# First gate weights loaded as words into the room of later tiles, and an opening written as one fixed list

## The chip, the cores and the metric

One NeuronCore of a Trainium2 chip runs the whole kernel. The metric is the device time of one launch in microseconds (us), taken as the median of several executions. Engines are named as in the profile: PE does the matmuls and the transposes through the identity, DVE the elementwise work on vectors, ACT the activations and copies, POOL little but the issue of loads, and SP issues most transfers.

## The reference

The three weight matrices are 64-bit floats, all other inputs 32-bit floats. There are 8 batches, 8 heads, 576 tokens and a head size of 64. Each head's keys and values are first condensed into 32 memory slots by a softmax over the tokens; the queries then attend to the 32 slots; the 4608 x 512 result goes through a gated feed-forward layer of width 1536.

```python
a = softmax(phi, axis=tokens)                     # (b, h, s, 32)
k_m = einsum('bhsm,bhsd->bhmd', a, k)             # 32 slots a head
v_m = einsum('bhsm,bhsd->bhmd', a, v)
attn = softmax(q @ k_m.T / 8) @ v_m               # (b, h, s, 64)
x = attn as (4608, 512)
out = (sigmoid(x @ w_gate) * (x @ w_val)) @ w_out # 512 -> 1536 -> 512
```

## The kernel before

**Weights.** The weights lie in memory as 64-bit words, two 32-bit integers each. The kernel turns them into 32-bit floats on the chip. `magnitude` lets ACT take the absolute value of the upper halves (L185), and `to_f32` then runs four DVE operations (L194 to L201): a clamp, a shift and mask, and two that put sign, exponent and low bits together. The 1536 columns are cut into twelve tiles f of 128. For each f there are three conversions of 128x512 numbers: (f, 0) and (f, 1) are the halves of the joint w_gate and w_val tile `wg[:, f]`, (f, 2) is the w_out tile, which is also split into `wo_hi` and `wo_lo` (L218 and L125). The words go through four rotating buffers named `words`. `CONVERT` says at which step each conversion is due; `load_jobs` issues the next load as soon as a buffer is free, by SP's queue in the opening and by POOL's later.

**Attention of one batch b.** `a_max` and `a_exp` make the softmax numerators of phi in place. `memory(b)` turns them by PE (nine transposes, copied by ACT into a tile named `e` and into `tails`), multiplies them with the keys and values `kvm` and `kvt` into one PSUM bank (80 small matmuls), scales by the reciprocal sums and turns the result into `kT` and `vT`. `scores` multiplies queries and `kT` for a cut c of the tokens (256 or 320), and DVE turns the result (L350). `s_max`, `s_exp` and `normalize` are the softmax on blocks of 32, `turned` turns it back (L396, L399), and `turn_hi` and `turn_lo` split it into `at_hi` and `at_lo`, each rounded so that three products hi-hi, hi-lo and lo-hi make up a full one.

**Feed-forward.** `make_u(b, fs)` multiplies `vT` with one or two tiles of `wg`, so that values and gate weights are joined, and splits the product into `u_hi` and `u_lo`. `gate_half(b, f, c)` then does twelve matmuls of `u` with `at` (gate and value, two halves, three products), ACT's sigmoid, DVE's product (L491), and its split into `g_hi` and `g_lo`. `out_half(b, f, c)` multiplies these with w_out into up to four accumulators `acc`, three half steps behind (LAG = 3). For batches 0 to 3 the tiles are done four at a time: steps 0 to 3 are batch 0 with tiles 0 to 3, steps 4 to 7 batch 1, steps 8 to 11 batch 2, steps 12 to 15 batch 3; then come batches 0 to 3 with tiles 4 to 7, then 8 to 11. After each four, sums go to memory as `part`. Batches 4 to 7 run through all twelve tiles at once.

**Order.** Matmuls keep their order in the program (`in_turn`), and so do table-bound activations (`curve`) and the transfers of each queue (`move`). A `step` or `piece` is put behind all that stands in the list so far, on PE, DVE, ACT and POOL. In the opening (L627 to L678) whole functions are listed, with `warm(n)` between them: n matmuls of the identity into a bank nobody reads. From step 0 on the loop at L755 works through the steps, and generators from `sides` run the attention of the next batch beside them. The opening ends with the second half of step 0; batch 1's attention lies beside steps 0 to 3, batch 2's beside steps 4 to 7, batch 3's beside steps 8 to 11. PSUM has eight banks: four `pu_t` in rotation, four `acc`, of which three join the rotation while the opening runs (`spread`).

Of the kernel before, what the change touches and what calls it, by code (L numbers as in the profile page):

```python
# [52 lines left out]
def attn_moe_kernel(
# [133 lines left out]
    def to_f32(f, k):  # L187


        if (f, k) not in sized:  # L190
# [10 lines left out]
        last_conv[0] = nc.vector.scalar_tensor_tensor(  # L201
            bits, low, 29, bits, op0=ALU.logical_shift_right, op1=ALU.bitwise_or
        )
# [7 lines left out]
        load_jobs(queue="batch" if spread else "stream")  # L211
        return dst

    def convert(f, k):
        dst = to_f32(f, k)
        if k == 2:
            hi, lo = wo_of(f)
            nc.scalar.copy(hi, dst)  # L218
# [49 lines left out]
    def memory(b):  # L268


        ph, z = loaded.pop((b, "phi")), loaded.pop((b, "z"))
        pf = ph.rearrange("p g s -> p (g s)")
        am = att([P, 2 * S], "e")[:, : NG * SF * P]
        am = am.rearrange("p (g c x) -> p g c x", g=NG, c=SF)
        for g in range(NG):
            pt = bank().rearrange("p (c x) -> p c x", c=SF)
            for c in range(SF):
                o = (g * (SF + 1) + c) * P
                transpose(pt[:, c, :], pf[:, o : o + P], ident)
            nc.scalar.copy(am[:, g], pt)  # L280
            yield
        pt = bank()
        transpose(pt[:, :P], pf[:, SF * P : (SF + 1) * P], ident)
        for g in range(NG):
            gs = slice(g * TAIL, (g + 1) * TAIL)
            nc.scalar.copy(tails[gs, g, :], pt[gs, :P])
        yield
        rz = att([P, NG], "rz")
# [1 line left out]
        nc.vector.reciprocal(rz, z)  # L290
        km, kt = loaded.pop((b, "kv"))
        kvp = bank().rearrange("p (g w d) -> p g w d", g=4, w=2)
        for g in range(NG):
# [20 lines left out]
        kvT = bank().rearrange("p (w g x) -> p w g x", w=2, g=NG)
        for g in range(NG):
            for w in range(2):
                transpose(kvT[:, w, g, :], kb[:, g, w].rearrange("p j d -> p (j d)"), ident)
        kvTs[b] = [keep.tile([P, NG, P], F32, name=f"{w}T", bufs=5 if w == "v" else 1) for w in "kv"]
        for w in range(2):
            nc.scalar.copy(kvTs[b][w], kvT[:, w])  # L320
# [107 lines left out]
    def make_u(b, fs):  # L428

# [7 lines left out]
        hi, lo = u_tiles()  # L437
        for r in range(2):
            nc.scalar.copy(hi[:, r, :nf], pb[r])  # L439
# [25 lines left out]
    def gate_half(b, f, c):  # L465
        hi, lo = U[b, f]
# [24 lines left out]
        last_prod[0] = nc.vector.tensor_tensor(prod[:, :n], ps[1][:, :n], sg[:, :n], op=ALU.mult)  # L491
# [354 lines left out]
```

## Time and profile before

| | |
|---|---|
| Time, median of three | 788.45 us (785.35 to 788.77) |
| Profiled execution, its own time | 786.25 us |
| Span of the profiled execution | 784.5 us |
| PE busy | 745.7 us (95%) |
| DVE busy | 436.6 us (56%) |
| ACT busy | 336.2 us (43%) |
| First gate matmul on PE | 30.64 us after the span's start |
| Begin of step 8 (batch 2) on PE | 121.95 us |

A group row gives source line, engine, operation, output and inputs with shapes, the count, the busy time and mean of one in ns, and the idle time of the engine ahead of it with what ended it. A timeline row gives start, duration, engine, line, operation and tiles, and in brackets the idle time ahead. A stage row gives, for a stretch of the span, its length, each engine's busy time and count, PE's granted clock, the share of the DMA engines and the rate in GB/s.

### The profile page before, as it was taken

The page shows a single profiled execution, that of the slowest core. Times are in us where ns is not written, and L with a number is a line of the kernel's source. Part 1 is how long each engine was busy: PE and PEld are TensorE (multiplying, and loading weights), DVE is VectorE, ACT ScalarE, POOL GpSimd, SP SyncE. Part 2 cuts the span into 40 slices and gives each one's busy share as a digit, 9 for nine tenths or more (in the row PEclk, how much of TensorE's full clock was granted, in tenths as well). Part 3 has the DMA queues.
Part 4 walks back from the last instruction along what each step waited for, and adds up shares of the span by engine and source line. Part 5 has one row for each costly group of instructions (what it writes and reads, how often), then busy time and mean ns, then how long its engine had stood idle before and what let it go on. Part 6 is the DMA issues. An engine that isn't in the chain of part 4 may idle for free.

```text
span 784.5 us, 13851 instructions
## 1 busy us (share of the span) xinstructions
PE 745.7 (95%) x5658; PEld 613.1 (78%) x5658; DVE 436.6 (56%) x840; ACT 336.2 (43%) x789; POOL 15.8 (2%) x34
## 2 busy tenths in 40 slices
PE   6866999989999999999999999999999999999997
PEld 4645777768888888887788878878888888888886
DVE  2889566977577775445554654365234553343432
ACT  3446455545544434332533443346333443333422
POOL 0001000001000000000000000000000000000000
PEclk8998899999999999999999999999999999999999
DMA  9683545664845654333253133002000100010002
GB/s 344 239 307 123 199 178 203 222 224 155 283 171 195 192 204 164 112 108 114 68 199 145 58 104 122 1 28 86 3 1 2 54 14 1 1 55 1 1 1 67
DMA packets 31231, 93.17 MB, mean 119 GB/s; under 512 B 3520, under 2 KB 4544, under 8 KB 29120
## 3 DMA queue, kind: packets, MB, share of 16 engines
q1 hardware_dynamic: 22528, 69.22, 24.4%
q0 software_dynamic: 4032, 14.68, 5.6%
q10 hardware_dynamic: 4608, 8.39, 3.6%
q8 instruction: 44, 0.72, 0.4%
q14 instruction: 19, 0.16, 0.1%
HBM read 69.73 MB, written 22.54 MB: 118 GB/s over the span
## 4 chain that ended last, share of the span: by engine, by line
PE 77%; DVE 9%; ACT 6%; DMA 4%; issue 2%; SPq 0%; ACTq 0%; DVEq 0%; POOLq 0%
PE pu_t L135 47%; PE acc L135 30%; DMA words<-in_wgv_dram 2%; ACT L110 2%; ACT ph L110 1%; DVE u_lo L125 1%; DVE q L396 1%; DVE e L375 1%; DVE sg L491 1%; DVE e L360 1%; ACT sg L110 1%; DVE at_lo L125 1%; DMA part<-row 1%; DMA out_dram<-row 1%; ACT e L110 1%
## 5 line engine op out<-in xcount | busy, mean ns | idle before, releaser
L135 PE MATMUL pu_t<-at_hi,u_hi 128*128 128x256 f32 (+1 forms) x760 | 229.1, 301 | 7.2 <-ACT u_hi L439 3.9
L135 PE MATMUL pu_t<-at_hi,u_lo 128*128 128x256 f32 (+1 forms) x760 | 225.0, 296 | 3.2 <-DVE u_lo L125 3.2
L135 PE MATMUL pu_t<-at_lo,u_hi 128*128 128x256 f32 (+1 forms) x760 | 225.2, 296 | 1.6 <-DVE at_lo L125 1.6
L491 DVE TENSOR_TENSOR sg<-pu_t,sg 128x256 f32<-128x256 f32 (+1 forms) x190 | 86.7, 456 | 202.8 <-ACT sg L110 129.6
L110 ACT ACTIVATE sg<-pu_t 128x256 f32<-128x256 f32 (+1 forms) x190 | 78.2, 412 | 224.3 <-PE pu_t L135 209.1
L135 PEld LDWEIGHTS pu_t<-at_hi,u_hi 128*128 128x128 f32 x760 | 144.2, 190 | 19.7 <-ACT u_hi L439 4.8
L135 PE MATMUL acc<-wo_hi,g_hi 128*128 128x512 f32 x384 | 157.1, 409 | 0.2 <-DVE row L517 0.2
L135 PE MATMUL acc<-wo_hi,g_lo 128*128 128x512 f32 x384 | 151.2, 394 | 0.0
L135 PE MATMUL acc<-wo_lo,g_hi 128*128 128x512 f32 x384 | 151.2, 394 | 0.0
L135 PEld LDWEIGHTS pu_t<-at_lo,u_hi 128*128 128x128 f32 x760 | 144.4, 190 | 8.3 <-DVE at_lo L125 1.8
L135 PEld LDWEIGHTS pu_t<-at_hi,u_lo 128*128 128x128 f32 x760 | 144.2, 190 | 4.1 <-DVE u_lo L125 4.1
L492 ACT CAST g_hi<-sg 128x256 fp32r<-128x256 f32 x192 | 78.0, 406 | 126.3 <-DVE sg L491 120.3
L125 DVE TENSOR_TENSOR g_lo<-sg,g_hi 128x256 fp32r<-128x256 f32 x192 | 80.9, 422 | 58.8 <-ACT g_hi L492 58.8
L135 PEld LDWEIGHTS acc<-wo_hi,g_hi 128*128 128x128 f32 x384 | 72.5, 189 | 49.5 <-issue 39.4
L135 PEld LDWEIGHTS acc<-wo_hi,g_lo 128*128 128x128 f32 x384 | 72.4, 189 | 17.2
L135 PEld LDWEIGHTS acc<-wo_lo,g_hi 128*128 128x128 f32 x384 | 72.5, 189 | 8.6
L125 DVE TENSOR_TENSOR u_lo<-pu_t,u_hi 128x512 fp32r<-128x512 f32 (+1 forms) x100 | 63.3, 663 | 3.6 <-ACT u_hi L439 2.3
L135 PE MATMUL pu_t<-wg,vT 64*32 64x512 f32 (+1 forms) x800 | 59.2, 596 | 5.8 <-DVE wg L201 5.2
L439 ACT CAST u_hi<-pu_t 128x512 fp32r<-128x512 f32 (+1 forms) x100 | 51.8, 570 | 2.6 <-PE acc L135 1.0
L517 DVE TENSOR_TENSOR row<-acc,row 128x512 f32<-128x512 f32 x32 | 21.9, 686 | 6.7 <-DMA row<-part 5.6
L110 ACT ACT_TABLE_LOAD x18 | 23.1, 1283 | 1.7 <-PEq L836 0.7
L135 PEld LDWEIGHTS pu_t<-wg,vT 64*32 64x32 f32 x800 | 10.3, 105 | 17.1 <-DVE wg L201 7.0
(93 smaller groups left out, 579.8 us busy)
## 6 DMA issues: line engine op xcount, KB each, us to landing
kvm<-in_kvm_dram SPq DMA_DIRECT2D x16, 1024.0 KB, 7.5
q<-in_qT_dram SPq DMA_DIRECT2D x16, 512.0 KB, 5.4
part<-row SPq DMA_DIRECT2D x32, 256.0 KB, 2.3
row<-part ACTq DMA_DIRECT2D x32, 256.0 KB, 2.8
out_dram<-row SPq DMA_DIRECT2D x32, 256.0 KB, 2.0
words<-in_wgv_dram POOLq DMA_DIRECT2D x12, 512.0 KB, 5.3
words<-in_wo_dram POOLq DMA_DIRECT2D x10, 512.0 KB, 5.2
ph<-in_phiT_dram SPq DMA_DIRECT2D x8, 576.0 KB, 4.0
```

Of the source, the lines that this page charges most:

```text
L110: last_act[0] = nc.scalar.activation(*args, **kw)
L125: return nc.vector.tensor_tensor(lo, x, hi.bitcast(F32), op=ALU.subtract)
L135: last_pe[0] = do(*args, **kw)
L360: nc.vector.tensor_tensor(e, e, mx.unsqueeze(3).broadcast_to([P, 2, w, M]), op=ALU.subtract)
L375: nc.vector.tensor_tensor(e, e, zs.unsqueeze(3).broadcast_to([P, 2, w, M]), op=ALU.mult)
L396: nc.vector.transpose(t.rearrange("p r n -> p (r n)"), loaded[b, "e"])
L439: nc.scalar.copy(hi[:, r, :nf], pb[r])
L491: last_prod[0] = nc.vector.tensor_tensor(prod[:, :n], ps[1][:, :n], sg[:, :n], op=ALU.mult)
L492: nc.scalar.copy(ghi, prod[:, : 2 * P])
L517: nc.vector.tensor_tensor(st, o, st, op=ALU.add)
```

## The change

Three things change.

First, the words of the w_gate tiles 0 to 3 no longer go through the `words` buffers. `load_gate(f)` loads all 1024 KB of a tile at once into `wg[:, 4 + 2f : 6 + 2f]`, the room of two later tiles, which is empty then. `gate_size` (ACT) and `gate_bits` (DVE) convert from there, tile 0 in two halves, tiles 1 to 3 in one go of 1024 columns. The w_out tiles 0 to 3 keep the four buffers.

Second, functions are split by engine (`scores` into `scores_of` on PE and `scores_turn` on DVE, `gate_half` into five, `make_u` into three, `memory` into its parts, and so on), and one text, `OPENING`, lists all operations of the steps 0 to 7, with the attention of batches 0 to 2, the first maximum of batch 3, the loads and the warm-ups. The loop begins at step 8. For batches 1 and 2 the phi numerators and the scaled keys get tiles of their own (`rooms`, three buffers of `left`) in place of `e`. U is made for two tiles at a time from the start.

Third, the conversions of tiles 4 to 6 are due at steps 11 to 15, up to two a step; before they were due at steps 7 to 15, one a step. From step 16 on nothing is moved.

```diff
+FIRST = 4
 CONVERT = {
-    -1: [(0, 0), (0, 1), (1, 0), (1, 1)], 0: [(0, 2), (2, 0), (2, 1)],
-    1: [(1, 2), (3, 0), (3, 1)], 2: [(2, 2)], 3: [(3, 2)], 7: [(4, 0)], 8: [(4, 1)], 9: [(4, 2)],
-    10: [(5, 0)], 11: [(5, 1)], 12: [(5, 2)], 13: [(6, 0)], 14: [(6, 1)], 15: [(6, 2)],
+    11: [(4, 0)], 12: [(4, 1), (4, 2)], 13: [(5, 0), (5, 1)], 14: [(5, 2), (6, 0)], 15: [(6, 1), (6, 2)],
...
+FIRST_U = [(0, [0, 1]), (0, [2, 3]), (1, [0, 1]), (1, [2, 3]), (2, [0, 1])]
+OPENING = """
+out 0; phi 0; gate 0; gate 3; gate 2; kvm 0 0; kvt 0; gate 1; kvm 0 1; ws 0; wb 0; amax 0; wh 0; wl 0;
+sz 0 0; sz 0 1; bt 0 0; aexp 0; bt 0 1; sz 3; W 42; T 0 0; T 0 2; T 0 1; Z 0; A 0 2; bt 3; phi 1;
+A 0 1; q 0 0; sz 2; q 0 1; A 0 0; W 23; K 0 0; bt 2; sz 1; bt 1; W 28; K 0 1; B 0; kvt 1; kvm 1 0;
+kvm 1 1; amax 1; W 5; t 0; V 0 0; V 0 1; W 2; S 0 0; aexp 1; U 0 0; tr 0 0; mx 0 0; S 0 1; uh 0 0;
+T 1 1; T 1 0; Z 1; A 1 1; T 1 2; ul 0 0; phi 2; A 1 0; q 1 0; A 1 2; out 3; ex 0 0; tr 0 1; q 1 1; W 7;
+K 1 0; out 2; nm 0 0; kvm 2 0; mx 0 1; W 8; K 1 1; B 1; kvm 2 1; tn 0 0; kvt 2; amax 2; ex 0 1; W 5;
+t 1; hi 0 0; V 1 0; nm 0 1; aexp 2; W 6; S 1 0; V 1 1; W 5; T 2 2; lo 0 0; T 2 1; A 2 2; S 1 1; tn 0 1;
+A 2 1; G 0 0 0; Z 2; hi 0 1; tr 1 0; lo 0 1; T 2 0; tr 1 1; U 0 2; sg 0 0 0; mx 1; A 2 0; G 0 0 1;
+uh 0 2; sg 0 0 1; G 0 1 0; gm 0 0 1; gm 0 0 0; ul 0 2; K 2 0; ex 1; G 0 1 1; gh 0 0 0; nm 1; K 2 1;
+sg 0 1 0; gh 0 0 1; G 0 2 0; B 2; kvt 3; out 1; gm 0 1 0; gl 0 0 0; gh 0 1 0; U 1 0; gl 0 0 1;
+sg 0 1 1; gl 0 1 0; sg 0 2 0; gm 0 1 1; G 0 2 1; uh 1 0; gm 0 2 0; tn 1; gh 0 1 1; t 2; sg 0 2 1;
+ul 1 0; G 0 3 0; hi 1; gm 0 2 1; V 2 0; O 0 0 0; lo 1; ws 1; V 2 1; G 0 3 1; gl 0 1 1; q 2 1; gh 0 2 0;
+wb 1; phi 3; sg 0 3 0; kvm 3 0; q 2 0; O 0 0 1; gl 0 2 0; wh 1; gm 0 3 0; G 1 0 0; sg 0 3 1; wl 1;
...
+"""
...
+    def early_words(f):
+
+        return wg[:, FIRST + 2 * f : FIRST + 2 * f + 2].rearrange("p f k n -> p (f k n)").bitcast(I32)
+
+    def load_gate(f):
+        move(early_words(f), wgv[f].rearrange("p k n -> p (k n)").bitcast(I32))
+
+    def gate_cut(f, k):
+
+        cut = slice(0, 1024) if k is None else slice(k * 512, k * 512 + 512)
+        words = early_words(f).rearrange("p (n t) -> p n t", t=2)
+        return wg[:, f].rearrange("p k n -> p (k n)")[:, cut], words[:, cut]
+
+    def gate_size(f, k=None):
+        dst, words = gate_cut(f, k)
+        nc.scalar.activation(dst, words[:, :, 1].bitcast(F32), AF.Abs)
+
+    def gate_bits(f, k=None):
+        last_conv[0] = bits_of(*gate_cut(f, k))
...
+    rooms.update(dict.fromkeys((1, 2), [mb.tile([P, TURN, P], F32, name="left", bufs=6) for _ in range(NG + 1)]))
+    halves = [mb.tile([P, 1024], F32, name=f"u_{w}", bufs=2) for w in ("hi", "lo")]
     warm(24)
-    step(a_max, 0)
-    step(a_exp, 0)
-    step(convert, 0, 0)
-    piece(m0, 3)
-    warm(8)
...
+    for word in OPENING.replace("\n", ";").split(";"):
+        if not word.split():
+            continue
+        name, *args = word.split()
+        if name == "O":
+            spread.clear()
+        ACTIONS[name](*map(int, args)) if name == "W" else step(ACTIONS[name], *map(int, args))
...
     sides = {
-        0: ([3, 3, 3, 2, 2, 1], m1, load(load_phi, 2), score(1, 2, load(load_kv, 2)), attend(1)),
-        begin[1, 0]: ([3, 3, 2, 2, 2, 1], remember(2, True), score(2, 3), attend(2)),
         begin[2, 0]: ([3, 3, 2, 2, 2, 1], remember(3, True), score(3), attend(3)),
...
+    pend = [(1, f, c, False, f == 3) for f in (2, 3) for c in range(2)][-LAG:]
     for i, (b, f, at_start, at_end) in enumerate(steps):
+        if i < DONE:
+            continue
```

In the list, `sz` and `bt` are the two parts of a w_gate conversion, `ws`, `wb`, `wh` and `wl` those of a w_out tile; `amax`, `aexp`, `T`, `A`, `Z`, `K`, `B`, `t` and `V` belong to the memory slots; `S`, `tr`, `mx`, `ex`, `nm`, `tn`, `hi` and `lo` to the attention; `U`, `uh` and `ul` to U; `G`, `sg`, `gm`, `gh` and `gl` to a gate half; `O` is an output half, `E` its copy from PSUM, `W n` are n warm-up matmuls, and `out`, `phi`, `gate`, `kvm`, `kvt`, `q` and `more` are loads. The numbers are batch, tile and cut. The part left out goes on in the same way to the last product of step 7, with w_out 2 and 3, batch 2's scores and softmax, and at its end the loads of batch 3's queries and keys.

More of the change, by code (lines that the diff above doesn't have):

```diff
@@ L210, in to_f32 @@
             pools["conv"] = ctx.enter_context(tc.tile_pool(name="conv1", bufs=1))
-        load_jobs(queue="batch" if spread else "stream")
+        load_jobs()
         return dst
@@ L266, in a_exp @@
         loaded[b, "z"] = z
[L268 to L288, printed above, removed]
-        nc.vector.tensor_scalar_add(z, z, EPS)
[L290 to L293, printed above, removed]
+    rooms = {}
@@ new lines, in phi_turn, with phi_copy @@
+    def phi_turn(b, g):
+        pf = loaded[b, "phi"].rearrange("p g s -> p (g s)")
+        pt = loaded[b, "pt", g] = bank()
+        for c in range(SF) if g < NG else range(1):
+            o = (g * (SF + 1) + c) * P if g < NG else SF * P
+            transpose(pt[:, c * P : (c + 1) * P], pf[:, o : o + P], ident)
+    def phi_copy(b, g):
+        pt = loaded.pop((b, "pt", g))
+        if g == NG:
+            for g in range(NG):
+                gs = slice(g * TAIL, (g + 1) * TAIL)
+                nc.scalar.copy(tails[gs, g, :], pt[gs, :P])
+            return
+        if (b, "am") not in loaded:
+            am = rooms.get(b)
+            if am is None:
+                am = att([P, 2 * S], "e")[:, : NG * SF * P].rearrange("p (g c x) -> p g c x", g=NG, c=SF)
+                am = [am[:, i] for i in range(NG)]
+            loaded[b, "am"] = am
+        nc.scalar.copy(loaded[b, "am"][g], pt.rearrange("p (c x) -> p c x", c=SF))
@@ L294, in memory, with phi_sum, keys @@
+    def phi_sum(b):
+        z = loaded.pop((b, "z"))
+        loaded[b, "rz"] = att([P, NG], "rz")
+        nc.vector.tensor_scalar_add(z, z, EPS)
+        nc.vector.reciprocal(loaded[b, "rz"], z)
+    def keys(b, gs=range(NG)):
+        am, kt = loaded[b, "am"], loaded[b, "kvt"]
+        if gs[0] == 0:
+            loaded[b, "kvp"] = bank().rearrange("p (g w d) -> p g w d", g=4, w=2)
+        kvp = loaded[b, "kvp"]
+        for g in gs:
+            km = loaded.pop((b, "kvm", g))
             for c in range(SF + 1):
@@ L312, in memory, with keys_turn, keys_keep @@
             )
-        yield
[L314 to L320, printed above, removed]
+        loaded[b, "kb"] = kb
+    def keys_turn(b):
+        kb = loaded.pop((b, "kb"))
+        kvT = loaded[b, "kvT"] = bank().rearrange("p (w g x) -> p w g x", w=2, g=NG)
+        for w in range(2):
+            for g in range(NG):
+                transpose(kvT[:, w, g, :], kb[:, g, w].rearrange("p j d -> p (j d)"), ident)
+    def keys_keep(b, ws=range(2)):
+        kvT = loaded[b, "kvT"]
+        if ws[0] == 0:
+            kvTs[b] = [keep.tile([P, NG, P], F32, name=f"{w}T", bufs=5 if w == "v" else 1) for w in "kv"]
+        for w in ws:
+            nc.scalar.copy(kvTs[b][w], kvT[:, w])
+    def memory(b):
+        for g in range(NG):
+            phi_turn(b, g)
+            phi_copy(b, g)
+            yield
+        phi_turn(b, NG)
+        phi_copy(b, NG)
+        yield
+        phi_sum(b)
+        keys(b)
+        yield
+        keys_copy(b)
+        yield
+        keys_turn(b)
+        keys_keep(b)
         yield
@@ L402, in turn_hi @@
     def turn_hi(b, c, t):
-        if not c:
+        if b not in at:
             new_at(b)
@@ L428, in make_u, with u_banks @@
     def make_u(b, fs):
+        u_banks(b, fs)
+        u_hi(b, fs)
+        u_lo(b, fs)
+    def u_banks(b, fs):
         nf = len(fs)
@@ L501, in out_half, with out_of @@
     def out_half(b, f, c, at_start, at_end):
+        out_of(b, f, c, at_start, at_end)
+        if at_end:
+            out_end(b, f, c)
+        if (b, f + 1) in ends and c:
+            for t in range(2):
+                rows[b, t] = row_of(b, t)
+    def out_of(b, f, c, at_start, at_end):
         hi, lo = G.pop((b, f, c))
```

248 lines of the change are left out of this document (144 added, 104 removed).

## The prediction, written before the result was known

> **What bounds the kernel now.** I read the page's slices first, then a table of busy time by stage.
>
> ```profile
> span 784.5 us, 13851 instructions
> ...
> PE   6866999989999999999999999999999999999997
> ...
> DVE  2889566977577775445554654365234553343432
> ```
>
> PE is full from the fifth slice on, but for one slice and the last, so only the front can give much; there DVE is the fuller engine.
>
> ```profile
> core 0: us, PE busy (x) PEld busy (x) DVE busy (x) ACT busy (x) POOL busy (x), PEclk, DMA share, GB/s
> 0.00:20.80 20.80, 13.25 (x161) 9.85 (x169) 4.17 (x9) 7.21 (x16) 0.70 (x6) 0.84 0.93 344
> 20.80:30.60 9.80, 6.17 (x77) 4.03 (x58) 8.52 (x19) 2.35 (x5) 0.00 (x0) 0.83 0.93 352
> 30.60:87.56 56.96, 43.81 (x398) 33.60 (x397) 49.28 (x94) 30.05 (x62) 3.84 (x8) 0.88 0.56 201
> 87.56:121.95 34.39, 33.28 (x319) 26.36 (x317) 21.15 (x37) 19.77 (x44) 0.52 (x1) 1.00 0.43 161
> 121.95:161.50 39.55, 34.24 (x319) 26.73 (x318) 31.05 (x57) 21.09 (x45) 2.11 (x4) 1.00 0.60 217
> 161.50:188.50 27.00, 26.72 (x171) 22.81 (x172) 19.08 (x40) 12.09 (x29) 2.11 (x4) 0.94 0.57 190
> 0.00:121.95 121.95, 96.51 (x936) 73.84 (x936) 83.11 (x158) 59.38 (x126) 5.05 (x14) 0.90 0.62 226
> ```
>
> The stages end where the timeline shows the marks below: first turn of the scores (20.8), first gate matmul (30.6), begin of batch 1's steps (87.56), of step 8, which is batch 2's first (121.95), of step 12 (161.5) and of step 16 (188.5).
>
> ```profile
> 2.60 0.74 SPq L121 DMA_DIRECT2D words<-in_wgv_dram  x1
> ...
> 12.40 0.66 ACT L185 ACTIVATE wg<-words 128x512 f32<-128x512 f32 x1 [5.22 <-DMA words<-in_wgv_dram]
> ...
> 13.59 1.93 PE L135 MATMUL pu_t<-kvm,e 128*32 128x128 f32 x32 [4.72 <-ACT e L280]
> ...
> 20.81 0.78 DVE L350 STREAM_TRANSPOSE e<-acc 128x256 f32<-128x256 f32 x2 [5.10 <-ACT wg L185]
> ...
> 30.64 0.36 PE L135 MATMUL acc<-at_hi,u_hi 128*128 128x256 f32 x1
> ...
> 121.95 0.38 PE L135 MATMUL pu_t<-at_hi,u_hi 128*128 128x256 f32 x1
> ```
>
> DVE works 4.17 of the first 20.8 us, then 49.28 of 56.96 (0.865), and only 21.15 of 34.39 (0.615) in batch 1's steps. So its work is badly spread. That PE pays for it is seen in its waits from 30.6 to 122, here the main ones (us in total, times, longest):
>
> ```profile
> PE pu_t L135 <- DVE sg L491: 4.0, 2, 3.8
> PE pu_t L135 <- ACT u_hi L439: 3.9, 2, 3.3
> PE pu_t L135 <- DVE u_lo L125: 2.7, 3, 1.5
> ...
> PE pu_t L135 <- DVE wg L201: 1.3, 1, 1.3
> ```
>
> The change replaces just this front, up to step 8, so I ask when step 8 starts in the new list (E; now 121.95), and then what the steps behind it do.
>
> **The change part by part.** *Loads and first score.* The same w_gate words now come in four loads of 1024 KB, all ahead of the last keys. Sizes and landing times of the first 60 us:
>
> ```profile
> kvm<-in_kvm_dram SPq DMA_DIRECT2D x6, 1024.0 KB, 7.6
> words<-in_wgv_dram SPq DMA_DIRECT2D x6, 512.0 KB, 10.5
> ...
> ph<-in_phiT_dram SPq DMA_DIRECT2D x3, 576.0 KB, 6.1
> words<-in_wo_dram SPq DMA_DIRECT2D x2, 512.0 KB, 6.8
> ...
> kvt<-in_kvt_dram SPq DMA_DIRECT2D x3, 256.0 KB, 4.2
> ```
>
> Up to the second half of batch 0's keys SP's queue now holds 512 (out 0) + 576 + 4 x 1024 (gates) + 2 x 1024 + 256 = 7488 KB = 7.67 MB. At 344 GB/s (first row of the table) that is 22.3 us. The first words load now has 576 + 256 + 2048 + 512 = 3392 KB = 3.47 MB up to its end, 10.1 us at that rate, and was waited for until 12.40, 2.3 later; so the keys are there between 22.3 and 24.6. From the first keys matmul (13.59) to the first turn (20.81) the kernel needs 7.2 us, in which half the keys, on a slow clock, take some 2; they are done ahead here. The first turn comes at 22.3 + 5 = 27 to 24.6 + 5 = 30; I take 28, **7 us later** than now.
>
> *What DVE has done by then.* Prices of one conversion's four operations, and wide against narrow ones:
>
> ```profile
> L198 DVE SCALAR_TENSOR_TENSOR wg<-words,wg 128x512 int32<-128x512 int32 x9 | 6.2, 691 | 0.2
> ...
> L201 DVE SCALAR_TENSOR_TENSOR wg<-words,wg 128x512 int32<-128x512 int32 x8 | 5.5, 689 | 0.2
> L254 DVE TENSOR_REDUCE nmx<-ph 128x2 f32<-128x1152 f32 x3 | 4.0, 1349 | 1.5 <-DMA ph<-in_phiT_dram 1.5
> L195 DVE TENSOR_SCALAR wg<-wg 128x512 int32<-128x512 int32 x9 | 3.8, 426 | 0.3
> L194 DVE TENSOR_SCALAR wg<-wg 128x512 f32<-128x512 f32 x9 | 3.8, 421 | 7.3 <-ACT wg L185 7.3
> ...
> L125 DVE TENSOR_TENSOR wo_lo<-wo_raw,wo_hi 128x512 fp32r<-128x512 f32 x4 | 2.7, 685 | 0.3 <-ACT wo_hi L218 0.3
> ...
> L375 DVE TENSOR_TENSOR e<-e,zs 128x1152 f32<-128x1152 f32 x2 | 2.7, 1350 | 0.0
> ...
> L375 DVE TENSOR_TENSOR e<-e,zs 128x512 f32<-128x512 f32 x1 | 0.7, 693 | 0.0
> ```
>
> Half a w_gate tile costs 0.69 + 0.69 + 0.43 + 0.42 = 2.23 us, a w_out tile 2.23 + 0.69 = 2.92. Gates 1 to 3 are now converted 1024 wide; from 693 to 1350 ns for 640 more columns, one operation of two saves 0.16, twelve at most 1.9: left out of the sum. Eight halves (17.8), w_out 0 (2.9) and two maxima (2.8) fit between the first words (about 7) and 28, beside DMA waits that nothing else fills. Of these only one half and the first maximum lie ahead of the first turn now. So of the 78.95 us that DVE is busy from 20.8 to 121.95 (8.52 + 49.28 + 21.15), 7 x 2.23 = 15.6, 2.92 and 1.35 go, as do the three operations of tile (4, 0) that ran before 121.95 (1.5): **57.6 us remain**.
>
> *From the first turn to the first gate matmul.* This takes 9.8 us now, 8.52 of them DVE's. The new list puts more ahead of it on DVE: all of the second half's maximum and normalization, batch 1's U and batch 2's maximum come or go against one conversion. I count 13 us (9.8 if it only moves, 16 if each handover waits): first gate at 41.
>
> *From there to step 8.* PE owes eight steps, one batch's keys and scores and four U pairs, less the three half products that stay pending, as now. The two stages that hold as much: batch 1's steps, 33.28 busy with a whole batch beside them, and steps 12 to 15, 26.72. A half product is 1.39:
>
> ```profile
> 175.16 1.39 PE acc L135 x6
> ```
>
> 33.28 + 26.72 - 4.17 = 55.8, so E is not before 41 + 55.8 = 96.8 by PE. By DVE: 28 + 57.6/0.865 = 94.6 at the best share of the table. Both near their limits at once will cost something: 34.39 - 33.28 = 1.1 us idle for four steps in the calm stage, and I take four times that, 4.3, for eight steps on a fuller DVE. **E = 101.1**, which is 57.6/73.1 = 0.79 of DVE's time, the share of steps 8 to 11 (31.05 of 39.55). The new list has 131 warm-up matmuls for 130, and they lie in waits as they did: nothing.
>
> *ACT.* The loads of its tables, up to step 8:
>
> ```profile
> L110 ACT ACT_TABLE_LOAD x6 | 7.7, 1283 | 0.8 <-PEq L836 0.7
> ```
>
> The new order goes from exponentials to sigmoids and back twice after the first gates: 8 loads for 6, 2.6 us. ACT is busy 59.38 of 121.95, and with some 62 of 101 it has room; between 0 and 2.6 of it can reach DVE's sums, and that is inside the 4.3.
>
> The Trainium skill (ScalarE: Activation LUTs, section Table sets: the hidden batching unit) says to batch activations by table set, which speaks against this order. By that rule the whole 2.6 would be lost and E would be 103.7; no run here shows yet which part of it is covered.
>
> *Private room for batches 1 and 2* (three tiles of `left` in place of `e`) costs no instruction. Its gain is that the keys needn't wait for the scores, and it is inside the 13.
>
> *Conversions put off.* Those of (4, 1), (4, 2), (5, 0), (5, 1) leave steps 8 to 11, and (4, 0) enters at 11. DVE there falls from 31.05 to 31.05 - 2 x 2.23 - 2.92 = 23.7, near batch 1's stage (21.15), which has the same work and took 34.39. The stage ends between 34.24 (its PE) and 39.55; I take 36.5, **3 gained**. Steps 12 to 15 get four more: 19.08 + 3 x 2.23 + 2.92 = 28.7 of DVE in 27.0 us. DVE becomes the limit there, at 28.7 (share 1.0) to 28.7/0.865 = 33.2; I take 31, **4 lost**. Their words come on POOL's queue two a step:
>
> ```profile
> words<-in_wgv_dram POOLq DMA_DIRECT2D x12, 512.0 KB, 5.3
> ```
>
> 5.3 us from issue to landing is under the 6.7 of a step, and they are asked for one step or more ahead: nothing.
>
> *Sum:* (101.1 - 121.95) - 3 + 4 = -19.9, and 786.25 - 19.9 = 766.4 against the profiled execution, which is 2.2 under the median of 788.45 and inside its runs. For the median I say **767**.
>
> **The rivals.** *A. SP's single line is late.* w_out 1 is now loaded behind batch 0's written-back halves and a keys load that waits for PE, and DVE meets its conversion in fixed order. What such a line costs now:
>
> ```profile
> 94.73 9.03 SPq L121 DMA_DIRECT2D part<-row  x4
> ...
> 141.23 4.01 DMA ph<-in_phiT_dram
> ```
>
> Four issues take 9.03 us, and one late load holds the chain for 4.01. Two such holds, for w_out 1 and batch 2's queries, give E = 109, DVE at 57.6/81 = 0.71 (steps 12 to 15 have 0.71): 774. For it: loads wait for work in the middle of the list. Against: by my sums the first loads are there at 25 and w_out 1 is wanted at about 60; at 352 GB/s, the second row's rate, 12 MB can come in between.
>
> *B. The put-off conversions take it back.* If DVE in steps 12 to 15 is only as dense as in batch 1's steps, 28.7/0.615 = 46.7, 19.7 more than now. With 3 gained at 8 to 11 this leaves 786.25 - 20.85 + 16.7 = 782, and a little more loss makes it no change. Against: there PE was the limit, so 0.615 wasn't DVE's best.
>
> *C. Slower: the fixed order stalls DVE.* Each maximum, exponential and normalization of batches 1 and 2 is one place in DVE's line, and whatever is behind waits for ACT's exponential and its table. The point is 0.615: 28 + 57.6/0.615 = 121.7, E as now. At 0.55 E = 132.7 and the time 798. For it: the first score is 7 us late for certain. Against: 0.865 was reached in the stage most like it.
>
> *D. Better than forecast:* PE's floor with no loss, E under 96, no loss at 12 to 15: about 757.
>
> **How the numbers follow.** What can be told from no change here is about 0.5%, 4 us. Forecast (first turn 27 to 30, E 95 to 107): 0.58, 759 to 773. A 0.18, up to 783. B 0.07. C 0.08. D 0.09. Faster: forecast, A and D, 0.85; same: B, 0.07; slower: C, 0.08. The range 756 to 780 leaves out C, B and the ends of A and D.
>
> **What would show it.** Right: DVE over 0.9 busy from about 8 to 27 us; the first score turn near 28 and the first gate matmul near 41, both later than now; step 8 near 101; DVE at 0.75 or more between; steps 12 to 15 some 4 us longer with PE waiting for DVE. Wrong: PE or DVE waiting for `words` or `q` loads between 45 and 80 (A), steps 12 to 15 over 40 us (B), DVE waiting for ACT's `e` for more than 15 us in all (C).

## The result, and the profile after

The changed kernel takes **761.79 us** (median of four, 761.44 to 762.09), the kernel before 787.53 (median of four, 785.35 to 788.77). The ratio is 0.9676, with a 95% interval of 0.9651 to 0.9701. The forecast of 767 was 5.2 too high and its range held the time. The profiled execution of the changed kernel took 762.09, its span 760.3; against the profile before (784.5) the span is 24.2 shorter.

The slices of the page of the changed kernel (tenths of busy time in 40 equal parts):

```profile
span 760.3 us, 13810 instructions
...
PE   7998999998999999999999999999999999999997
...
DVE  7897748995777754456646533365333743343422
```

Before, DVE began with 2 and 8 and PE was below 9 in its first four slices and needed until the fifth to fill up. Now DVE works from the first slice on, and PE is at 9 from the second on but for the fourth, the tenth and the last.

The changed kernel by stages, cut at the marks that are shown below (columns as in the prediction), and a last row for the stretch in which most of the early words are converted:

```profile
core 0: us, PE busy (x) PEld busy (x) DVE busy (x) ACT busy (x) POOL busy (x), PEclk, DMA share, GB/s
0.00:29.93 29.93, 24.56 (x241) 18.97 (x249) 21.56 (x31) 12.55 (x23) 1.37 (x7) 0.89 0.89 351
29.93:43.16 13.23, 11.56 (x225) 8.10 (x209) 12.88 (x26) 8.99 (x24) 0.00 (x0) 1.00 1.01 398
43.16:101.82 58.66, 55.31 (x482) 45.20 (x471) 48.66 (x88) 39.25 (x78) 1.59 (x3) 0.97 0.55 200
101.82:135.30 33.48, 32.49 (x319) 26.36 (x317) 20.13 (x33) 17.82 (x37) 0.00 (x0) 1.00 0.52 195
135.30:163.40 28.10, 26.96 (x178) 22.46 (x177) 26.73 (x58) 15.20 (x36) 3.99 (x7) 1.00 0.70 232
9.00:28.00 19.00, 15.28 (x170) 12.23 (x168) 17.16 (x24) 7.82 (x15) 0.00 (x0) 0.82 0.94 379
```

The kernel before, cut in the same way at its first gate matmul and at its step 8:

```profile
0.00:30.64 30.64, 19.46 (x223) 13.91 (x224) 12.72 (x28) 9.56 (x21) 0.70 (x6) 0.83 0.93 347
30.64:121.95 91.31, 77.05 (x716) 59.93 (x713) 70.39 (x131) 49.82 (x105) 4.36 (x8) 0.93 0.51 186
```

The marks in the changed kernel's timeline: second half of batch 0's keys, first turn of the scores, first gate matmul, begin of steps 8, 12 and 16:

```profile
25.79 1.08 PE L160 MATMUL pu_t<-kvm,e 128*32 128x128 f32 x32
...
29.93 0.78 DVE L467 STREAM_TRANSPOSE e<-acc 128x256 f32<-128x256 f32 x2 [1.73 <-PE acc L160]
...
43.16 0.39 PE L160 MATMUL pu_t<-at_hi,u_hi 128*128 128x256 f32 x1
...
101.82 0.28 PE L160 MATMUL pu_t<-at_hi,u_hi 128*128 128x256 f32 x1
...
135.25 0.39 PE L160 MATMUL pu_t<-at_hi,u_hi 128*128 128x256 f32 x1
...
163.40 0.28 PE L160 MATMUL pu_t<-at_hi,u_hi 128*128 128x256 f32 x1
```

So the 24.2 us come from these places. Step 8 begins at 101.82 for 121.95: **-20.1**. Steps 8 to 11 take 33.4 for 39.55: **-6.1**. Steps 12 to 15 take 28.2 for 27.0: **+1.2**. The rest, from step 16 on, takes 596.9 (760.3 - 163.4) for 596.0 (784.5 - 188.5): **+0.9**.

The first of these has two halves that pull against each other. The first gate matmul comes 12.5 us *later* (43.16 for 30.64). But the stretch from there to step 8 is 32.7 us shorter (58.66 for 91.31). It holds 482 PE instructions for 716, for two reasons. The list has batch 1's keys and scores done ahead of the first gate, where PE issues some 450 instructions for 220. And 64 of the 716 are warm-ups, while the changed kernel has none behind its first gate. Here are 56 of them in the kernel before; they fill PE's wait for the second half of step 0, whose softmax was not yet done:

```profile
32.49 6.29 PE L135 MATMUL acc<-ident 128*128 128x256 bf16 x56
```

PE idles 3.4 us in the stretch (58.66 - 55.31) for 14.3 (91.31 - 77.05), so 10.9 of the 32.7 us are idle time that is gone. The other 21.7 us are busy time that is gone: 7.3 of it are the 64 warm-ups, which do no work, and the rest is work moved ahead or run at a faster clock (0.97 for 0.93).

One wait of PE is left between the first gate and step 8. Its rows in the wait table and in the timeline:

```profile
PE pu_t L160 <- ACT left L652: 3.3, 1, 3.3
```

```profile
75.51 1.11 PE L160 MATMUL pu_t<-q,kT 64*32 64x256 f32 x16 [3.35 <-ACT left L652]
...
77.14 0.63 PE L160 MATMUL acc<-wo_lo,g_hi 128*128 128x512 f32 x1
...
82.34 0.39 PE L160 MATMUL acc<-wo_lo,g_hi 128*128 128x512 f32 x1
```

It is put down to ACT, but ACT had long been free: the instruction is the first score of batch 2, whose first queries were issued as the last of SP's line (63.91) and landed 11.5 us later. Behind the gap the same matmul takes 0.63 us for 0.39.

### The profile page after: what moved, and what is told of

It is laid out like the page before. It is cut to its first block, busy times and chain, and to the rows that moved or that the text cites. A ratio compares the mean times of both kernels' runs of the same rounds, so it can differ in the third digit from the quotient of the medians.

```text
span 760.3 us, 13810 instructions
## 1 busy us (share of the span) xinstructions
PE 737.1 (97%) x5651; PEld 610.0 (80%) x5651; DVE 434.6 (57%) x824; ACT 337.6 (44%) x784; POOL 14.1 (2%) x30
## 4 chain that ended last, share of the span: by engine, by line
PE 86%; ACT 4%; DVE 4%; DMA 3%; issue 1%; SPq 0%; DVEq 0%; ACTq 0%
PE pu_t L160 51%; PE acc L160 35%; DMA kvm<-in_kvm_dram 2%; ACT L135 2%; ACT ph L135 1%; DMA part<-row 1%; DVE q L513 1%; ACT sg L135 0%; DMA row<-part 0%; DVE u_lo L150 0%; DVE sg L636 0%; DVE e L492 0%; DVE g_lo L150 0%; SPq L146 0%; DVE at_lo L150 0%
## 5 line engine op out<-in xcount | busy, mean ns | idle before, releaser
L160 PEld LDWEIGHTS pu_t<-at_lo,u_hi 128*128 128x128 f32 x760 | 142.7, 188 | 6.5
L160 PEld LDWEIGHTS pu_t<-at_hi,u_lo 128*128 128x128 f32 x760 | 142.5, 187 | 1.5 <-DVE u_lo L150 1.5
L150 DVE TENSOR_TENSOR g_lo<-sg,g_hi 128x256 fp32r<-128x256 f32 x192 | 80.6, 421 | 56.0 <-ACT g_hi L647 55.8
L150 DVE TENSOR_TENSOR u_lo<-pu_t,u_hi 128x512 fp32r<-128x512 f32 x93 | 60.6, 684 | 3.8 <-ACT u_hi L567 2.6
L160 PE MATMUL pu_t<-wg,vT 64*32 64x512 f32 x744 | 52.8, 601 | 2.8 <-DVE wg L248 2.8
L567 ACT CAST u_hi<-pu_t 128x512 fp32r<-128x512 f32 x93 | 49.9, 587 | 5.3 <-PE pu_t L160 3.6
L160 PE MATMUL acc<-ident 128*128 128x256 bf16 x155 | 23.0, 313 | 1.4 <-POOL ident masks.py:199 1.4
```

Of the source, the lines that this page charges most:

```text
L150: return nc.vector.tensor_tensor(lo, x, hi.bitcast(F32), op=ALU.subtract)
L160: last_pe[0] = do(*args, **kw)
L567: nc.scalar.copy(U[b, fs[0]][0][:, r, :nf], pb[r])
```

## The experiments

All kernels ran beside the kernel before, which took 786.6 to 786.9 us (medians) beside them.

**The early words alone, in the old order.** The kernel before, with four loads into the later tiles' room and all conversions of tiles 0 to 3 right behind the first maximum:

```diff
-    -1: [(0, 0), (0, 1), (1, 0), (1, 1)], 0: [(0, 2), (2, 0), (2, 1)],
-    1: [(1, 2), (3, 0), (3, 1)], 2: [(2, 2)], 3: [(3, 2)], 7: [(4, 0)], ...
+    0: [(0, 2)], 1: [(1, 2)], 2: [(2, 2)], 3: [(3, 2)], 7: [(4, 0)], ...
...
     load_phi(0)
+    load_gate(0)
+    load_gate(3)
+    load_gate(2)
     load_kv(0)
+    load_gate(1)
...
-    step(convert, 0, 0)
+    step(gate_size, 0)
+    step(gate_bits, 0)
     piece(m0, 3)
+    (gate_size and gate_bits of 3, 2 and 1, between warm-ups)
```

> The kernel before with one part of the change alone: the words of the first four w_gate tiles are loaded into the room of later tiles and all converted in the opening, right behind the first maximum; the conversions of steps 0 to 3 and of the opening fall away, the order of all else is the old one, (4, 0) and later are converted at their old steps. Theory (the gain comes from DVE's idle time at the front, which the early words fill): the conversions of 15.6 us leave the stretch from the first turn to step 8, which holds at most that; the first turn comes 7 to 9 us later as in the changed kernel, so 5 to 9 us of the 20 are left, and what is still missing is the order's: 774 to 778 us against 787. Rival (the fixed list is the source, the words alone only push the first score back): 784 to 792.

Measured: 786.98 us (782.59 to 788.41, ten runs), ratio 0.9998 [0.9981, 1.0016]. No difference: my theory of the time, that filling DVE's idle front is the gain by itself, **falls** for this kernel. But the zero is a sum of two things. Its stages, cut at its first gate matmul and its step 8:

```profile
0.00:37.52 37.52, 27.60 (x309) 21.31 (x309) 22.71 (x34) 12.13 (x22) 0.70 (x6) 0.86 0.96 386
37.52:123.11 85.59, 76.61 (x713) 60.02 (x713) 59.42 (x109) 46.95 (x101) 2.25 (x4) 0.92 0.43 154
```

DVE lost 11.0 us of work in the stretch (59.42 for 70.39), as it should, and the stretch became 5.7 shorter (85.59 for 91.31). But the first gate comes 6.9 later. Counted from the first turn of the scores, 8.9 us are gained behind it (92.27 for 101.14 up to step 8) and 10.0 lost ahead of it (30.84 for 20.81). And this kernel's late first turn is in part its own doing:

```profile
20.08 0.40 PE L135 MATMUL pu_t<-kvt,tails 128*32 128x128 f32 x8
...
26.66 0.16 DVE L318 TENSOR_SCALAR z<-z 128x2 f32<-128x2 f32 x1
...
27.14 0.84 ACT L336 ACTIVATE e<-pu_t,rz 128x256 f32<-128x256 f32 x2 [4.37 <-DVE rz L319]
...
30.84 0.78 DVE L379 STREAM_TRANSPOSE e<-acc 128x256 f32<-128x256 f32 x2 [3.81 <-PE acc L135]
...
40.31 7.95 PE L135 MATMUL acc<-ident 128*128 128x256 bf16 x56
```

PE is done with the keys at 20.5, but the reciprocal sums that scale them stand on DVE behind all conversions, the last of which waits for tile 1's words; in the changed kernel the reciprocal is done at 14. I estimate from these rows that with the reciprocal ahead, the first turn would come at 24 to 25: 3.8 us from the reciprocal to the turn, counted from 20.5, and the first queries landed at 22.9. What that saves, up to 6 us less the conversion of tile 1 (3.8) that then lies later, was not tried. So that the early words are worth nothing alone is shown for this order only. Nor does PE's own work fill the stretch: of the 76.6 us that PE is busy in it, 9.0 are the 64 warm-ups (56 of them in the last row), as in the kernel before.

**The list, with half of the early conversions late.** In the changed kernel, the bits of tiles 3 and 2 wait until the first gates. The loads, and the bits of tiles 0 and 1, stay early, so this isn't the list quite alone; a kernel with nothing early in the list was not tried.

```diff
-... A 0 2; bt 3; phi 1;
+... A 0 2; phi 1;
-... K 0 0; bt 2; sz 1; bt 1; W 28;
+... K 0 0; sz 1; bt 1; W 28;
-... lo 0 1; T 2 0; tr 1 1; U 0 2;
+... lo 0 1; bt 3; bt 2; T 2 0; tr 1 1; U 0 2;
```

> The changed kernel with the integer operations of w_gate tiles 3 and 2 (two times 3.83 us of DVE) moved out of the first 28 us to the place just ahead of the turned phi and U of batch 0's second pair. The words are loaded and sized as early as before. Theory (DVE between the first turn and step 8 decides, and its idle time at the front is what the change uses): the 7.7 us come back at 0.84 or so of DVE's share, between 4 and 9 us: 766 to 770 against 762. Rival (from the first gate on PE alone decides; it is 94% busy from 41 to 102): no more than the 1 or 2 us that PE is idle there, 762 to 763.5.

Measured: 770.69 us (769.71 to 771.82), ratio 0.9797 [0.9768, 0.9825], 8.9 above the changed kernel and just above the theory's 766 to 770. Its stage from the first gate to step 8, and PE's waits from 41 to 111:

```profile
42.18:110.97 68.79, 57.79 (x482) 46.90 (x472) 56.33 (x96) 39.44 (x78) 1.58 (x3) 0.90 0.46 172
```

```profile
PE pu_t L160 <- DVE wg L248: 7.7, 1, 7.7
PE pu_t L160 <- ACT left L652: 3.3, 1, 3.3
```

The 7.7 us of bits come back as one wait of 7.7, and the rest as a slower clock behind it (0.90 for 0.97 in the stretch). Was that only the lump? The next kernel spreads them and puts U of tiles 2 and 3 off:

```diff
-... tr 1 1; U 0 2; sg 0 0 0; mx 1; A 2 0; G 0 0 1;
-uh 0 2; sg 0 0 1; G 0 1 0; gm 0 0 1; gm 0 0 0; ul 0 2; K 2 0; ex 1; G 0 1 1; gh 0 0 0; nm 1; K 2 1;
+... tr 1 1; sg 0 0 0; mx 1; A 2 0; G 0 0 1;
+sg 0 0 1; G 0 1 0; gm 0 0 1; gm 0 0 0; bt 3; K 2 0; ex 1; G 0 1 1; gh 0 0 0; bt 2; nm 1; U 0 2; K 2 1; uh 0 2; ul 0 2;
```

> As the kernel with the bits of w_gate tiles 3 and 2 late (770.7 us), but no longer in one lump ahead of the first gates' next U: bt 3 stands behind the first gate's products, bt 2 behind the first halves of step 0, and U of tiles 2 and 3 only ahead of step 2, where it is wanted. Theory (DVE's work between the first gate and step 8 decides: 48.7 of 58.7 us there and 7.7 more would be 0.96 of it, so that most of it has to show): 766 to 770. Rival (only the lump cost time, PE waited once for 7.7 us; spread out it finds cover): 761.5 to 764.

Measured: 771.54 us (769.15 to 773.05), ratio 0.9799 [0.9777, 0.9822]: above both expectations, and no better than the lump. PE's waits from 28 to 112:

```profile
PE pu_t L160 <- DVE wg L248: 4.6, 1, 4.6
PE pu_t L160 <- DMA q<-in_qT_dram: 4.4, 1, 4.4
```

The wait for the bits is smaller (4.6) but still there, and the one for the queries is a microsecond longer, which I hadn't reckoned with. The kernels side by side:

| | first turn | from there to step 8 | step 8 |
|---|---|---|---|
| the kernel before | 20.81 | 101.14 | 121.95 |
| early words, old order | 30.84 | 92.27 | 123.11 |
| the list, bits of tiles 2 and 3 late, in a lump | 29.17 | 81.80 | 110.97 |
| the same, spread | 29.98 | 81.57 | 111.55 |
| the changed kernel | 29.93 | 71.89 | 101.82 |

Behind the first turn, early conversions pay in both orders: 8.9 us in the old one, for 15.6 us of DVE's work moved ahead, and 9.7 to 9.9 in the list, for 7.7 us. So they are worth more in the list, though a part of that is where the late bits were put, just ahead of a product that wants them. The largest difference is the list's own: 20.4 us behind the first turn between two kernels that both have the early words (92.27 and 71.89). The kernel before isn't the old order with the same bits late, since it has tile 1 and half of tile 0 late too and its first turn early. So how much of the 20.1 us the list would give with nothing early stays open.

**Batch 2's first queries ahead of the other loads.**

```diff
-... q 2 1; gh 0 2 0;
-wb 1; phi 3; sg 0 3 0; kvm 3 0; q 2 0; O 0 0 1; ...
+... q 2 0; q 2 1; gh 0 2 0;
+wb 1; sg 0 3 0; phi 3; kvm 3 0; O 0 0 1; ...
```

> The loads of batch 2's queries stand ahead of batch 3's phi and keys instead of behind them; nothing else is moved. Theory (late load): in the changed kernel PE waits 3.35 us at 72.2 for these queries, which took 11.5 us to land, and its clock is halved for some 5 us behind that; both go, so 757 to 759 us against 761.8, and step 8 begins 3 to 5 us before 101.8. Rival (DVE is what fills the stretch, the wait only moves to the next product): 761 to 762.

Measured: 757.9 us (755.33 to 758.32), ratio 0.9634 [0.9617, 0.965]. Of PE's waits between 38 and 96 only two of 0.2 are left:

```profile
PE pu_t L160 <- ACT kT L413: 0.2, 1, 0.2
PE acc L160 <- ACT ph L135: 0.2, 1, 0.2
```

The wait that the table put down to ACT was the queries' load. In the medians it cost 3.9 us, of which the gap is 3.35; the slow matmuls behind it are the likely rest. (In the profile step 8 begins 5.3 earlier, at 96.48, but 1.0 of that is there at the first turn already, ahead of the edit. And the matmuls behind the gap were slow for 3.4 us, not for the 5 that I had written.)

**Tile 4's words in SP's line.** In the changed kernel the load that `more` issues is POOL's, and POOL runs ahead of its place in the list. The row of the changed kernel, on POOL:

```profile
7.94 0.67 POOL L146 DMA_DIRECT2D words<-in_wgv_dram  x1 [6.63 <-DVE wo_raw L248]
```

```diff
-"more": load_jobs,
+"more": lambda: load_jobs(queue="batch"),
```

> The words of tile 4 are loaded by SP's queue at their place in the list instead of by POOL's, which issued the first of them at 7.94 us, far ahead of that place. Theory (the 512 KB lie between batch 0's keys): the second half of the keys is there 1.5 us earlier than 25.8, and batch 2's queries no longer share the engines with two more loads of 512 KB: 758 to 760 us. Rival (neither is on the path): 761 to 762.

Measured: 756.84 us (755.82 to 757.05), ratio 0.9616 [0.9601, 0.963]. Its second half of the keys and its first turn:

```profile
22.84 1.08 PE L160 MATMUL pu_t<-kvm,e 128*32 128x128 f32 x32 [2.53 <-DMA kvm<-in_kvm_dram]
...
26.98 0.78 DVE L467 STREAM_TRANSPOSE e<-acc 128x256 f32<-128x256 f32 x2
```

Both are 3.0 earlier (25.79 and 29.93 before), and the time is better than the theory had it. The size of the 3.0 is less sure: in the four profiles with the same list up to there and POOL's early load the first turn lies at 28.8 to 30.2, in the five with the load in line at 27.0 to 27.6. The two edits together:

> Both orders of loads together. Theory: 755 to 758 us, the two gains mostly add up. Rival: 761 to 762; or, if only one of the two counts, the time of that one.

Measured: 755.6 us (753.36 to 756.54), ratio 0.9598 [0.9579, 0.9618]. The gains don't add (3.9 and 5.0 against 6.2): with the words in line the first edit has less left to remove, as PE waits 1.2 us for queries there and not 3.3.

**The conversions of tiles 4 to 6 at their old steps.** The one part of the change that lies behind step 8, undone:

```diff
-    11: [(4, 0)], 12: [(4, 1), (4, 2)], 13: [(5, 0), (5, 1)], 14: [(5, 2), (6, 0)], 15: [(6, 1), (6, 2)],
+    8: [(4, 0), (4, 1)], 9: [(4, 2)], 10: [(5, 0)], 11: [(5, 1)], 12: [(5, 2)], 13: [(6, 0)], 14: [(6, 1)], 15: [(6, 2)],
```

> The new opening, but the conversions of tiles 4 to 6 at steps 8 to 15 about one a step, nearly as in the kernel before ((4, 0) and (4, 1) at 8, which were at 7 and 8). Theory (putting them off pays because batch 3's attention needs DVE at steps 8 to 11): steps 8 to 11 grow from 33.5 us by 3.5 to 6, steps 12 to 15 shrink by 1, the time is 764 to 767 us. Rival (the gain of steps 8 to 11 came from the state the opening leaves): 761 to 762.

Measured: 763.08 us (762.29 to 763.82), ratio 0.9697 [0.9683, 0.9712], only 1.3 above the changed kernel: between theory and rival, and the two intervals touch. Its stages from step 8 to 12 and 12 to 16:

```profile
100.53:139.30 38.77, 34.27 (x319) 26.54 (x317) 29.21 (x54) 21.08 (x44) 2.11 (x4) 1.00 0.62 218
139.30:168.99 29.69, 28.91 (x176) 24.56 (x177) 20.34 (x42) 12.98 (x32) 2.49 (x5) 0.89 0.53 182
```

That is 68.5 us for the changed kernel's 61.6, 6.9 more, with step 8 beginning 1.3 earlier. Steps 8 to 11 grew by 5.3, as the theory has it; steps 12 to 15 didn't shrink but grew by 1.5. At the first sigmoid of step 16 it is 5.6 behind, and at that of step 40 only 1.4. The two sigmoids of the kernel with the old steps, then those of the changed kernel:

```profile
170.60 0.39 ACT L135 ACTIVATE sg<-pu_t 128x256 f32<-128x256 f32 x1 [1.43 <-PE pu_t L160]
...
334.26 0.39 ACT L135 ACTIVATE sg<-pu_t 128x256 f32<-128x256 f32 x1 [1.41 <-PE pu_t L160]
```

```profile
165.01 0.39 ACT L135 ACTIVATE sg<-pu_t 128x256 f32<-128x256 f32 x1 [1.02 <-PE pu_t L160]
...
332.82 0.39 ACT L135 ACTIVATE sg<-pu_t 128x256 f32<-128x256 f32 x1 [1.41 <-PE pu_t L160]
```

So putting off leaves a debt. The largest wait of it is U's for the last bits of tile 7, here in the changed kernel; with the old steps the same wait is 0.3:

```profile
175.89 1.06 PE L160 MATMUL pu_t<-wg,vT 64*32 64x512 f32 x8 [2.81 <-DVE wg L248]
```

**A middle way**, put on the kernel with both load edits:

```diff
-    11: [(4, 0)], 12: [(4, 1), (4, 2)], 13: [(5, 0), (5, 1)], 14: [(5, 2), (6, 0)], 15: [(6, 1), (6, 2)],
+    10: [(4, 0)], 11: [(4, 1), (4, 2)], 12: [(5, 0)], 13: [(5, 1), (5, 2)], 14: [(6, 0), (6, 1)], 15: [(6, 2)],
```

> The kernel with batch 2's first queries ahead and tile 4's words in SP's line (755.6 us), with six of the nine put-off conversions one step earlier: (4, 0) at 10, (4, 1) and (4, 2) at 11, (5, 0) at 12, (5, 1) and (5, 2) at 13, (6, 0) and (6, 1) at 14, (6, 2) at 15. Theory (the put-off conversions leave a debt: those of tile 7 come late at steps 16 to 18, where PE waits 2.8 us for DVE's bits of wg and 1.4 for row, which the kernel with conversions at their old steps doesn't have): the wait goes, 1 to 3 us gained, 752.5 to 754.5. Rival (DVE is full from step 11 on, and whatever comes earlier pushes PE's work back by as much): 755.5 to 757.

> The kernel with batch 2's first queries ahead, tile 4's words in SP's line and six conversions a step earlier, once more and unchanged, beside the others on one chip: 754.5 to 756.5 (755.4 before).

Measured: 755.41 us (753.87 to 757.4), ratio 0.961 [0.9577, 0.9643], and once more 754.86 (753.79 to 755.61), ratio 0.9589 [0.9575, 0.9603]. In the trace the debt is gone: U's wait for the bits is 0.3 for 2.8, and the span is 751.6 for 753.8. In the medians 0.2 to 0.7 us of it are seen, which these runs can't tell from nothing.

```profile
PE pu_t L160 <- DVE wg L248: 0.3, 1, 0.3
```

**Fewer table loads.** Batch 3's phi exponential goes right behind batch 2's exponential of the scores, first in the changed kernel, then in the middle way:

```diff
-tr 2 0; aexp 3; wb 3; S 2 1;
+tr 2 0; wb 3; S 2 1;
-E 0 3 0 0; O 0 3 1; gl 1 0 1; ex 2; G 1 2 1;
+E 0 3 0 0; O 0 3 1; gl 1 0 1; ex 2; aexp 3; G 1 2 1;
```

> The changed kernel with batch 3's phi exponential moved right behind batch 2's exponential of the scores, so that ACT loads its tables six times up to step 8 and not eight (two times 1.28 us fewer). By the sum of the prediction the loads lie beside PE's work: 761 to 762, as the changed kernel. The Trainium skill (ScalarE: Activation LUTs, section Table sets: the hidden batching unit) would have the 2.6 us saved: 759.

> The kernel with batch 2's first queries ahead, tile 4's words in SP's line and six conversions a step earlier (755.4 us), and batch 3's phi exponential right behind batch 2's exponential of the scores, so two table loads fewer on ACT up to step 8. Here no load of queries is late beside it. By the covered sum: within 1.5 us of 755.4. By the Trainium skill (ScalarE: Activation LUTs, section Table sets: the hidden batching unit): the two loads of 1.28 us saved, 753. If the exponential itself is wanted where it stands (batch 3's slots come later behind it), 757 to 759.

Measured: 765.69 us (761.23 to 767.53), ratio 0.9724 [0.9683, 0.9765], and 753.69 (752.85 to 756.31), ratio 0.9581 [0.9559, 0.9602]. The first says nothing on tables. PE's wait for batch 2's queries lies in the same place and was longer in its profiled execution, and so was the slow clock behind it:

```profile
76.74 1.11 PE L160 MATMUL pu_t<-q,kT 64*32 64x256 f32 x16 [4.41 <-DMA q<-in_qT_dram]
...
81.88 0.58 PE L160 MATMUL pu_t<-at_hi,u_hi 128*128 128x256 f32 x1
```

In the second, where that wait is gone, ACT loads six tables up to step 8:

```profile
L135 ACT ACT_TABLE_LOAD x6 | 7.7, 1283 | 0.8 <-PEq L990 0.7
```

Its 1.2 us below the same kernel with eight (754.86) is inside what both intervals leave open, and step 8's first sigmoid is 1.5 later in it (97.45 for 95.97), 0.7 of which is there at the first gate already, ahead of the edit. Whether the two loads cost anything stays open; that they cost the whole 2.6 isn't what was measured.

**Without the later warm-ups.** The 89 warm-up matmuls behind the first phi's transposes are left out:

```diff
-A 0 1; q 0 0; sz 2; q 0 1; A 0 0; W 23; K 0 0; bt 2; sz 1; bt 1; W 28; K 0 1; ...
+A 0 1; q 0 0; sz 2; q 0 1; A 0 0; K 0 0; bt 2; sz 1; bt 1; K 0 1; ...
 (and W 5, W 2, W 7, W 8, W 5, W 6 and W 5 further on)
```

> The changed kernel with only the first 66 warm-up matmuls; the 89 that stand between the first phi's transposes and the first gate matmul are left out. Theory (as the prediction has it: they lie in waits that something else sets, and what they cost and keep warm is nothing in sum): 760.5 to 763. Rival 1 (they hold PE's clock: without them the keys' and scores' matmuls of batches 0 and 1 run at half clock, and the first gate comes 2 to 5 us later): 764 to 768. Rival 2 (the 38 that stand between the first score and the first gate, some 4 us of PE, are on the path): 758 to 760.

Measured: 766.44 us (764.61 to 768.71), ratio 0.9729 [0.9709, 0.975], 4.65 above the changed kernel. Two stretches of its front, 12 to 29 and 29 to 44 us, and then those of the changed kernel:

```profile
12.00:29.00 17.00, 6.04 (x91) 4.42 (x95) 14.57 (x18) 5.17 (x11) 0.00 (x0) 0.61 0.96 370
29.00:44.00 15.00, 10.51 (x178) 6.25 (x178) 12.50 (x25) 9.70 (x24) 0.00 (x0) 0.73 0.89 319
```

```profile
12.00:29.00 17.00, 13.10 (x148) 9.96 (x145) 14.51 (x18) 5.19 (x11) 0.00 (x0) 0.80 0.92 357
29.00:44.00 15.00, 13.22 (x248) 9.44 (x249) 13.69 (x30) 10.75 (x27) 0.00 (x0) 1.00 1.01 401
```

But for the warm-ups PE has the same work to do, and its clock is 0.61 and 0.73 for 0.80 and 1.00. The first gate matmul comes at 45.65 for 43.16. A part of the 4.65 is later waits for queries, 7.8 us in two for 3.3 in one; that part is not the clock's, or not directly, and how the 4.65 divides is not shown:

```profile
PE pu_t L160 <- DMA q<-in_qT_dram: 7.8, 2, 4.6
```

**The private room** for batches 1 and 2 is in every kernel with the list. By my reading of the list, batch 1's numerators in `e` would close a circle of waits in its fixed order; no run shows it, and what the room is worth stays open.

## Why the prediction was right, point by point

| Step | Predicted | Measured |
|---|---|---|
| First turn of the scores | 28 | 29.93 |
| First gate matmul | 41 | 43.16 |
| From there to step 8 | 60.1 (PE 55.8 and 4.3 idle) | 58.66 (PE 55.31 and 3.35 idle) |
| Step 8 (E) | 101.1 | 101.82 |
| Steps 8 to 11 | 36.5 | 33.4 |
| Steps 12 to 15 | 31 | 28.2 |
| From step 16 on | 0 | +0.9 |

- **The front.** DVE was to be over 0.9 busy from about 8 to 27, and is at 17.16 of 19.00 from 9 to 28. E was right to 0.7. The floor by PE (55.8) was right within 1 us, and so was the idle time (4.3), but that one by luck: I took it as what PE and DVE cost each other when both are near their limits, and the 3.35 us measured are one wait for queries, rival A's cause. No wait of PE for DVE shows in the stretch. With both loads mended E is 95.17.
- **The first turn was mis-sized by 2 us.** I summed SP's queue up to the keys and left out POOL's: its 512 KB stand late in the list, but POOL has nothing to do and issues them at 7.94. In SP's line the first turn is at 26.98, a little ahead of my 27 to 30.
- **DVE's remaining work was mis-sized:** 57.6 predicted, 12.88 + 48.66 = 61.5 measured. The operations that went were counted rightly. What I didn't count is what the list does ahead of step 8 that the old loop did behind it: by their counts, U's low parts for a pair more, one product and the low parts of two, 1.9 us. The other 2 us I can't place. The share at which DVE can run was mis-sized as well (0.79 predicted; 61.5 of 71.9 is 0.86), and the two errors cancel. The prediction by PE was the sounder one.
- **The reason that I gave was the smaller part of it.** "Its work is badly spread" reads as if the early words were the gain. Alone, in the one order that was tried, they come to nothing (786.98): 8.9 us gained behind the first turn, 10.0 lost ahead of it. The larger part is the list's, 20.4 us behind the first turn against that kernel: batch 1's keys and scores go ahead of the first gate, where PE had waited, and the waits that 64 warm-ups filled behind it are gone. How the 20.4 divide among these two, U made for two tiles at a time and the private room is not shown. I had this in one clause under the PE floor. None of my rivals had it.
- **Warm-ups: the step "nothing" failed,** twice. There are 155 and not 131 in the new opening (24 stand ahead of the list), and they do more than fill a wait: without the last 89 the kernel takes 4.65 us more.
- **Conversions put off:** both stages were mis-sized by 3 us, in one direction. For steps 8 to 11 I took the stage between the 34.24 that PE was busy there before and 39.55. But that busy time is no floor: with less on DVE the same 319 instructions take 32.49, at the same clock of 1.00. In steps 12 to 15 DVE reaches 0.95 (26.73 of 28.10), and so near no loss. What I took as -3 and +4 is -6.1 and +1.2 in the trace. By the kernel with the old steps, though, it is only 1.3 in the end: steps 16 on pay most of it back, which I had at nothing.
- **Rival A** was there in small: one hold of 3.35 on the queries that it names. It costs 3.9, not the 8 it was given for two, and w_out 1 was not late. **B**, steps 12 to 15 over 40, didn't come: 28.2. **C** didn't: DVE has no wait for ACT's `e` from 28 to 102. **D** would be the kernel with both loads mended: 755.6, near its 757, with E at 95.17, under its 96.
- **Tables:** eight loads up to step 8, as counted, and ACT at 60.8 busy (62 predicted). The rule of the Trainium skill (ScalarE: Activation LUTs, section Table sets: the hidden batching unit) is neither borne out nor refuted by the 1.2 us between the two kernels of the middle way.

The fastest kernels here are the middle way with eight or six table loads, 754.9 and 753.7 us, 7 to 8 us below the changed kernel and 4% below the kernel before; the kernel with the two load edits alone (755.6) can't be told from them.

## What to carry to other kernels

Before work is moved off a busy helper engine, look at both ends of the move: taking 11 us from DVE's busy stretch made all behind the first turn 8.9 us shorter, and the same work at its new place put the first turn 10.0 later, in part because a small operation that the next stage needed stood behind it. When a zero comes out, split it at such a mark before the cause is dropped. Don't read dummy matmuls as work when a busy share is taken for a limit. In a fixed order, read every queue's loads in the order in which its engine can reach them and not in the order of the text, since an idle engine issues its load at once and in front of what is wanted first. And look behind a stage that got faster by postponing work: the steps after it may pay it back.

## What the runs showed of the hardware that I had not expected

- **A gap of 3.35 us on PE costs twice.** After it the same 128x512 matmul takes 0.63 us for 0.39, and full speed is back at about 79, 3.4 us later. After 4.41 us, in the first kernel with fewer table loads, the slow stretch lasted longer, from 76.7 to about 82.5. The Trainium skill (TensorE: Matmul & The Clock Gate, section Why this matters for your kernels) warns of idle gaps of over some 3 us between matmuls; this trace agrees. The dummy matmuls in the front are worth their place: with 89 of them left out, the clock there was 0.61 and 0.73 for 0.80 and 1.00, and the kernel took 4.65 us more.
- **A load on another queue isn't behind the line.** 512 KB on POOL's queue, issued at 7.94 us while SP's loads of words and keys were under way, landed 9.9 us later, ahead of keys that SP had issued before them; with them in SP's line the first turn comes 1 to 3 us earlier (27.0 to 27.6 for 28.8 to 30.2). The Trainium skill (DMA: Bandwidth & Descriptors, section Queues, rings and completion order) says that a DMA engine takes turns between the queues that have work, by packets; the trace agrees so far as POOL's load didn't wait for SP's earlier ones.
- **The operations of a conversion cost less than double when twice as wide, but not equally.** Of the four, the masks and shifts with two inputs go from 692 to 1225 ns for double the columns, those with one input from 428 to 694:

```profile
L245 DVE SCALAR_TENSOR_TENSOR wg<-wg 128x1024 int32<-128x1024 int32 x3 | 3.7, 1225 | 0.1
...
L242 DVE TENSOR_SCALAR wg<-wg 128x1024 int32<-128x1024 int32 x3 | 2.1, 694 | 0.1
...
L245 DVE SCALAR_TENSOR_TENSOR wg<-wg 128x512 int32<-128x512 int32 x2 | 1.4, 692 | 0.1
L242 DVE TENSOR_SCALAR wg<-wg 128x512 int32<-128x512 int32 x2 | 0.9, 428 | 0.1
```

A w_gate tile is thus converted in 3.83 us for 2 x 2.23, 0.6 saved for each of three tiles.
